# Decode attention with gated mix on one core: two V pairs loaded in halves, and the V sums in two PSUM tiles

## The chip, the core and the metric

One core of a Trainium2 chip. The metric is the device time of one execution in microseconds, lower is better; 2% is the threshold for "faster" or "slower". Engines: PE (TensorE matmul), PEld (its weight load), DVE (VectorE), ACT (ScalarE), POOL (GpSimd), SP (SyncE, which issues nearly all transfers here). The program uses one core. "Granted clock" is the share of its full clock at which PE was let run: 1.00 is called warm, 0.50 cold or half clock. PSUM is the memory, in banks, into which PE adds up its products. "Debt" is the time by which PE ends late because its own work, and not a transfer, holds it up. The "span" is the length of an execution as its profile shows it.

## The reference

Four decode queries attend over caches of 8192 positions and 32 heads; a small gated MLP runs beside it; the two results are mixed.

```
q      = (x @ wq)                                  # x [4,1,1024], 32 heads of 128
scores = q · k_cache * 128**-0.5                   # k_cache [4,32,8192,128] bf16, 256 MiB
o      = softmax(scores) · v_cache                 # v_cache the same size
a      = o @ wo                                    # wo [4096,1024], 8 MiB
b      = x + routed gated MLP(x)                   # w_gate, w_up, w_down 7 MiB each
out    = g * a + (1 - g) * b,   g = sigmoid(sum(x * gate_w))
```

Nearly all bytes, 512 MiB of 549, are the two caches.

## The kernel before

The caches come in "pairs": four heads, 8 MiB, two slots of a ring of five slots. K pairs 0 to 31 and V pairs run interleaved, V eight pairs behind; behind the last K pair only V pairs 24 to 31 (and 23) remain. A pair comes as one transfer, or as two halves where it wraps round the ring; the last three V pairs come in smaller pieces. PE adds a V pair in 64 matmuls into four PSUM banks; behind every second (odd) pair, ScalarE and VectorE add the four banks up into `OS`.

```python
def load_pair(src, n, apart=False):
    a = slots(2)
    if a + 1 < NS and not apart:              # one transfer of 8 MiB
        lo = a * RING
        nc.sync.dma_start(out=flat[:, lo:lo + 2 * n], in_=src)
        return [flat[:, lo:lo + n], flat[:, lo + n:lo + 2 * n]]
    halves = [ring[:, a], ring[:, (a + 1) % NS]]
    ...                                       # two transfers of 4 MiB

o_ps = accp.tile([P, 4, NB], F32, name="o_ps")   # four banks, one tile

def v_pair(d):
    flush_sums()
    if d < ND - 3:                            # ND = 32
        vs = load_pair(vv, RING)
    else:
        ...                                   # pairs 29 to 31: halves and smaller pieces
    for u in range(4 * RD):                   # 16 x 4 matmuls
        n, z = divmod(u, 4)
        vn = vs[n // JT]
        for w in range(4):
            nc.tensor.matmul(o_ps[row:row + NM, w, :], ...)
        if u == 1:
            flush()                           # small matmuls on OS
    if tv == GV - 1:                          # odd pairs
        sum_up(g, t, b, h0)

def sum_up(g, t, b, h0):
    nc.scalar.activation(out=OS[:], in_=o_ps[:, 0, :], func=ACT.Copy, scale=mE[:, 0:1])
    def sums():
        for w in range(1, 4):
            nc.vector.scalar_tensor_tensor(out=OS[:], in0=o_ps[:, w, :], scalar=mE[:, w:w + 1], in1=OS[:], ...)
    full.append(sums)
```

At the end: two blocks of `wo` (1 MiB each) ahead of pair 31, six behind it, the last two in pieces; each block is eight matmuls. Then a cast and the output transfer.

Of the kernel before, what the change touches and what calls it, by code (L numbers as in the profile page):

```python
# [9 lines left out]
F32 = mybir.dt.float32  # L10
U32 = mybir.dt.uint32
ACT = mybir.ActivationFunctionType
ALU = mybir.AluOpType
# [99 lines left out]
def kernel(  # L113
# [15 lines left out]
    nc = tc.nc  # L129
    P = 128  # L130
    Bn, Sq, D = A_x.shape
    _, H, Sk, Dh = A_k_cache.shape
# [8 lines left out]
    GD = QP // RD  # L141
    GH = GD * NQ
    ND = Bn * H // NQ
# [4 lines left out]
    FR = 4  # L148
    FG = F // (P * FR)
    NB = 512  # L150
    NH = D // NB
    RING = JR * Dh
# [3 lines left out]
    scale = float(Dh) ** -0.5  # L156
# [6 lines left out]
    accp = ctx.enter_context(tc.tile_pool(name="accp", bufs=1, space=PSUM))  # L163
# [14 lines left out]
    def turned(rows, n, dtype=BF):  # L178
        t = TB[tb_turn[0] % 3]
        tb_turn[0] += 1  # L180
        return t[0:rows, 0:n] if dtype == BF else t[0:rows, 0:2 * n].bitcast(dtype)

    def slots(n):
        at = turn[0]
        turn[0] = (at + n) % NS
        return at
# [3 lines left out]
    def load_pair(src, n, apart=False):  # L190

        a = slots(2)
        if a + 1 < NS and not apart:
# [4 lines that stand above are left out]
        for i, half in enumerate(halves):  # L198
            nc.sync.dma_start(out=half[:, 0:n], in_=src[:, i * n:(i + 1) * n])
        return halves  # L200


    S0 = scp.tile([P, 4, NB], F32, name="S_ps")
    o_ps = accp.tile([P, 4, NB], F32, name="o_ps")

    def bank(ps, z, shape, dtype=F32):
        b = ps[:, z] if dtype == F32 else ps[:, z].bitcast(dtype)
        n = 1
        for k in shape:
            n *= k  # L210
        names = "abcd"[:len(shape)]
        return b[:, 0:n].rearrange("p (%s) -> p %s" % (" ".join(names), " ".join(names)), **dict(zip(names, shape)))
# [8 lines left out]


    q_ps = S0[:, 0:2]
    for z in (q_ps, o_ps[:, 0:2], o_ps[:, 2:4]):
        nc.vector.memset(z, 0.0)

    row = const.tile([P, 2, 32], F32)
# [21 lines left out]
    for half in range(2):  # L249
        for e in range(2):  # L250
            nc.gpsimd.tensor_copy(out=R[:, 2 * half + e].rearrange("p (n j) -> p n j", n=4),
                                  in_=ident[:, 64 * half + e:64 * half + 64:2].unsqueeze(1).to_broadcast([P, 4, 32]))
# [7 lines left out]
    mE = const.tile([P, 4], F32)  # L260
# [9 lines left out]
    OS = const.tile([P, 4 * Dh], F32)  # L270
# [9 lines left out]
    A_ps = []  # L280
# [33 lines left out]
    def x_rows(ps, ws, nb, cols):  # L314

        for half, w in enumerate(ws):
            for t in range(TW):
                for k in range(4):
                    for z in range((nb - k + 3) // 4):
                        nc.tensor.matmul(ps[32 * k:32 * k + Bn, z, :], lhsT=xT[TW * half + t], rhs=cols(w, t, 4 * z + k),  # L320
                                         start=(half + t == 0), stop=(half == 1 and t == TW - 1), skip_group_check=True)
# [19 lines left out]
    def gu_piece(view, w_i):  # L341

        ws = load_pair(view.rearrange("(c t) f -> c (t f)", t=DT), TW * F)

        def cols(w, t, i):
            row = w[:, t * F:(t + 1) * F].rearrange("p (f i r) -> p f i r", i=FG, r=FR)
            return row[:, :, i, :]
        x_rows(o_ps[:, 2 * w_i:2 * w_i + 2], ws, FG, cols)

    def h_done():  # L350
        h = turned(P, 1024, F32).rearrange("p (z n) -> p z n", z=2)
        nc.scalar.activation(out=h, in_=o_ps[:, 0:2], func=ACT.Silu)
        nc.vector.tensor_tensor(out=h, in0=h, in1=o_ps[:, 2:4], op=ALU.mult)
        for z in range(2):
            ht = bank(o_ps, z, [FR, 4, 32])
            for r in range(FR):
                nc.tensor.transpose(out=ht[:, r].rearrange("p k i -> p (k i)"), in_=h[:, z, r:512:FR], identity=ident[:])
            kn = min(4, FG - 4 * z)
            for r in range(FR):
                nc.vector.tensor_tensor(out=hT[:, 4 * z:4 * z + kn, r, :], in0=ht[:, r, 0:kn, 0:Bn],  # L360
                                        in1=c12[:, 1:2, :].to_broadcast([P, kn, Bn]), op=ALU.mult)
# [46 lines left out]
    full = []  # L408
    ahead = []

    def flush():
        while pending:
            pending.pop(0)()

    def flush_sums():
        while full:
            full.pop(0)()

    def flush_late():
        while late:  # L420
            late.pop(0)()

    def heads(d):
        return divmod(d * NQ, H)

    def kv_view(cache, d):
        b, h0 = heads(d)
        return cache[b, h0:h0 + NQ].rearrange("h (r j) d -> (h r) (j d)", j=2 * JR)
# [86 lines left out]
    NM = 16 * NQ  # L515

    def v_pair(d):
        b, h0 = heads(d)
        g, t = divmod(d, GD)
        tv = t % GV  # L520
        row = NM * tv
        flush_sums()
        vv = kv_view(A_v_cache, d)
        if d < ND - 3:
            vs = load_pair(vv, RING)
        else:
            vs = [ring[:, slots(1)] for _ in range(2)]
            for half, cuts in ((0, 1), (1, 2)) if d < ND - 1 else ((0, 2), (1, 4)):
                for c in range(cuts):
                    lo, hi = c * RING // cuts, (c + 1) * RING // cuts  # L530
                    nc.sync.dma_start(out=vs[half][:, lo:hi], in_=vv[:, half * RING + lo:half * RING + hi])
        for u in range(4 * RD):
            n, z = divmod(u, 4)
            vn = vs[n // JT]
            for w in range(4):
                j0 = CJ * (n % JT) + 16 * z + 4 * w
                nc.tensor.matmul(o_ps[row:row + NM, w, :],  # L537
                                 lhsT=PB[:, RD * (d % NW) + n, z].rearrange("p w s j -> p (w s j)"),
                                 rhs=vn[:, j0 * Dh:(j0 + 4) * Dh], start=(u == 0), stop=(u == 4 * RD - 1),
                                 skip_group_check=True)  # L540
            if u == 1:
                flush()
            if u == 7:
                flush_late()
        if tv == GV - 1:
            sum_up(g, t, b, h0)
        if t < GD - NW:
            spread_p(d + NW)
        if t == GD - 1 and d + 1 < ND:
            spread_p(d + NW)  # L550

    def sum_up(g, t, b, h0):
        nc.scalar.activation(out=OS[:], in_=o_ps[:, 0, :], func=ACT.Copy, scale=mE[:, 0:1])  # L553

        def sums():
            for w in range(1, 4):
                nc.vector.scalar_tensor_tensor(out=OS[:], in0=o_ps[:, w, :], scalar=mE[:, w:w + 1], in1=OS[:],  # L557
                                               op0=ALU.mult, op1=ALU.add)
        full.append(sums)

        def finish():
            ps = A_ps[1] if A_ps else o_ps
            oT = bank(ps, 0, [HV])
            for q in range(4):
                nc.tensor.matmul(oT, lhsT=OS[:, q * Dh:(q + 1) * Dh], rhs=selg[:, q].rearrange("p t s -> p (t s)"),  # L565
                                 start=(q == 0), stop=(q == 3), skip_group_check=True)
            if t == GV - 1:
                tot = bank(ps, 1, [GH])
                nc.tensor.matmul(tot, lhsT=rs_t[g][:, 0:1].to_broadcast([P, P]), rhs=mask, start=True, stop=True, skip_group_check=True)

            def scaled():
                if t == GV - 1:
                    rinv_t[g] = stat.tile([P, GH], F32, name="rinv", tag="rinv")
                    nc.vector.reciprocal(out=rinv_t[g][:], in_=tot)
                hg = h0 + NQ - HV
                at = NQ * t + NQ - HV
                nc.vector.scalar_tensor_tensor(out=OT[:, hg:hg + HV, b], in0=oT, scalar=sgb[:, 1, b:b + 1],  # L577
                                               in1=rinv_t[g][:, at:at + HV], op0=ALU.mult, op1=ALU.mult)
            late.append(scaled)
        pending.append(finish)  # L580
# [3 lines left out]
    q_done()  # L584
    gates()
    gu_piece(B_w_gate, 0)
    side = {1: lambda: (gu_piece(B_w_up, 1), h_done())}
    GE = NWB - HV // WB
    order = []
# [70 lines left out]
```

## Time and profile before

| | before |
|---|---|
| time, median of 3 runs | 1343.73 us (1342.73 to 1343.86) |
| time of the run whose profile was read | 1345.62 us |
| span of that profile | 1343.8 us |
| transfers' share of the span | 99.3% |

The chain that ended last shows how the end came about (start, length, what):

```profile
1229.08 29.40 DMA ring<-in_A_v_cache_dram
1258.48 0.14 issue
1258.62 2.56 PE o_ps L537 x8
...
1335.71 5.14 PE acc L286 x23
```

From the landing of pair 28 at 1258.48 on, the end follows PE (and the sums that it waits for), and no transfer. The other lines of this profile are in the prediction.

### The profile page before, as it was taken

The numbers are of one execution on the slowest core, as the hardware profiler recorded it, in microseconds if no ns is written. First come the engines' busy times: TensorE is split into PE (matmuls) and PEld (weight loads), VectorE is DVE, ScalarE is ACT, GpSimd is POOL, SyncE is SP. The second block draws the span as 40 slices with busy tenths as digits, with TensorE's granted clock in tenths as the row PEclk, the third lists the DMA queues.
The fourth block names the chain that finished last, engine by engine and source line by source line (L and its number), as shares of the span: only waits on it lengthen the run. The fifth ranks groups of instructions, "written<-read, shape, count | busy, mean of one in ns | idle before, by whom it ended". The sixth has DMA issues, their size and how long they took to land.

```text
span 1343.8 us, 6898 instructions
## 1 busy us (share of the span) xinstructions
PE 1063.6 (79%) x4608; PEld 139.9 (10%) x1396; DVE 638.9 (48%) x386; ACT 63.3 (5%) x94; POOL 71.6 (5%) x209
## 2 busy tenths in 40 slices
PE   2665877897878789787879778789588878888898
PEld 0000000011010011101001010101001010111111
DVE  2555988556544347455436256646135556000001
ACT  0000000200000000100000000100000000100000
POOL 2000000100000001000000000100000000100000
PEclk9687999898989899888889889889898889888889
DMA  9999999999999999999999999999999999999997
GB/s 414 445 421 436 438 433 423 444 434 423 438 437 425 435 435 427 440 436 430 435 432 431 437 435 422 436 429 434 437 424 445 433 422 436 434 424 438 424 425 303
DMA packets 14602, 576.13 MB, mean 429 GB/s; under 512 B 1630, under 2 KB 1638, under 8 KB 2284
## 3 DMA queue, kind: packets, MB, share of 16 engines
q1 hardware_dynamic: 14564, 575.69, 99.3%
q8 instruction: 23, 0.38, 0.1%
q14 instruction: 7, 0.06, 0.0%
q10 hardware_dynamic: 8, 0.00, 0.0%
HBM read 575.68 MB, written 0.01 MB: 428 GB/s over the span
## 4 chain that ended last, share of the span: by engine, by line
DMA 59%; DVE 23%; PE 16%; another core or an unknown queue 1%; issue 0%; ACT 0%; SPq 0%; DVEq 0%
DMA ring<-in_A_k_cache_dram 51%; DVE TB L453 20%; PE o_ps L537 12%; DMA ring<-in_A_v_cache_dram 7%; DVE OS L557 2%; PE S_ps L458 2%; DMA x<-in_gate_w_dram 2%; PE acc L286 1%; PE led L565 0%; PE S_ps L320 0%; DVE PT L494 0%; DVE mx L480 0%; ACT OS L553 0%; PE o_ps L565 0%
## 5 line engine op out<-in xcount | busy, mean ns | idle before, releaser
L453 DVE STREAM_TRANSPOSE TB<-ring 128x2048 uint32<-128x2048 uint32 x256 | 568.1, 2277 | 472.2 <-DMA ring<-in_A_k_cache_dram 453.6
L458 PE MATMUL S_ps<-TB,Z 128*128 128x512 bf16 x2048 | 530.5, 413 | 189.1 <-DVE TB L453 181.5
L537 PE MATMUL o_ps<-ring,PB 128*64 128x512 bf16 x2048 | 469.7, 392 | 48.9 <-DMA ring<-in_A_v_cache_dram 39.5
L458 PEld LDWEIGHTS <-Z 128*128 128x128 bf16 x512 | 53.0, 103 | 651.7 <-issue 651.7
L537 PEld LDWEIGHTS <-PB 128*64 128x64 bf16 x512 | 57.7, 113 | 453.2 <-issue 452.5
L557 DVE SCALAR_TENSOR_TENSOR OS<-o_ps,mE,OS 128x512 f32<-128x512 f32 x48 | 35.6, 741 | 141.6 <-ACT OS L553 140.5
L513 POOL COPY PB<-PT 32x256 bf16<-32x256 bf16 x64 | 39.0, 609 | 720.3 <-PE o_ps L537 527.2
L511 ACT COPY PB<-PT 32x256 bf16<-32x256 bf16 x64 | 39.6, 618 | 254.3 <-PE o_ps L537 248.5
L435 POOL COPY Z<-qa 32x4 bf16<-32x4 bf16 x128 | 25.7, 201 | 458.5 <-PE S_ps L458 432.0
L553 ACT ACTIVATE OS<-o_ps,mE 128x512 f32<-128x512 f32 x16 | 11.0, 687 | 592.1 <-PE o_ps L537 592.1
L489 ACT ACTIVATE TB<-S_ps,mx 128x2048 bf16<-128x2048 f32 x4 | 7.9, 1967 | 321.2 <-DVE mx L486 321.2
L286 PE MATMUL acc<-ring,hT 128*4 128x512 bf16 x56 | 14.2, 421 | 5.4 <-ACT TB L489 5.4
L244 PE MATMUL S_ps<-identb,x 6*128 6x6 bf16 x8 | 0.6, 195 | 22.2 <-DMA x<-in_gate_w_dram 22.2
L286 PE MATMUL acc<-ring,LT 128*4 128x512 bf16 x64 | 14.4, 379 | 0.4 <-DVE LT L383 0.4
L320 PE MATMUL o_ps<-ring,xw 128*4 128x512 bf16 x112 | 10.1, 483 | 4.6 <-DMA ring<-in_B_w_gate_dram 4.6
L565 PEld LDWEIGHTS o_ps<-selg,OS 128*128 128x128 f32 x88 | 11.5, 191 | 9.4 <-issue 9.0
L494 DVE STREAM_TRANSPOSE PT<-TB 128x2048 bf16<-128x2048 bf16 x4 | 9.2, 2311 | 6.4 <-ACT TB L489 6.4
L480 DVE TENSOR_REDUCE mx<-S_ps 128x1 f32<-128x2048 f32 x4 | 9.1, 2281 | 6.2 <-PE S_ps L458 6.2
L565 PE MATMUL o_ps<-selg,OS 128*128 128x8 f32 x88 | 10.5, 245 | 0.0
L577 DVE SCALAR_TENSOR_TENSOR OT<-led,sgb,rinv 128x8 bf16<-128x8 f32 x5 | 1.2, 236 | 15.4 <-PE led L565 15.3
L383 DVE CAST LT<-led 128x96 bf16<-128x96 f32 (+1 forms) x2 | 0.4, 224 | 15.9 <-PE led L381 15.9
L246 DVE COPY xw<-S_ps 128x48 bf16<-128x48 bf16 x1 | 0.2, 181 | 15.7 <-PE S_ps L244 15.7
(68 smaller groups left out, 73.6 us busy)
## 6 DMA issues: line engine op xcount, KB each, us to landing
ring<-in_A_k_cache_dram SPq DMA_DIRECT2D x14, 4096.0 KB, 33.4
ring<-in_A_v_cache_dram SPq DMA_DIRECT2D x14, 4096.0 KB, 28.9
ring<-in_A_v_cache_dram SPq DMA_DIRECT2D x6, 2048.0 KB, 26.7
ring<-in_B_w_gate_dram SPq DMA_DIRECT2D x1, 7168.0 KB, 37.1
ring<-in_B_w_up_dram SPq DMA_DIRECT2D x1, 7168.0 KB
ring<-in_B_w_down_dram SPq DMA_DIRECT2D x1, 7168.0 KB
ring<-in_A_wo_dram SPq DMA_DIRECT2D x6, 1024.0 KB, 26.4
ring<-in_A_v_cache_dram SPq DMA_DIRECT2D x4, 1024.0 KB, 27.0
```

The costliest lines, as they stand in the source:

```text
L286: nc.tensor.matmul(acc(n), lhsT=lhsT, rhs=rhs, start=start, stop=True, skip_group_check=True)
L320: nc.tensor.matmul(ps[32 * k:32 * k + Bn, z, :], lhsT=xT[TW * half + t], rhs=cols(w, t, 4 * z + k), start=(half + t == 0), stop=(half == 1 ...
L435: nc.gpsimd.tensor_copy(out=Z[at, :, QP - 1 + QP * q], in_=qa[at, :, h0 + q, b])
L453: nc.vector.transpose(out=flat_t.bitcast(U32).rearrange("p (j i) -> p j i", j=CJ), in_=kn[:, half].bitcast(U32))
L458: nc.tensor.matmul(sps[:, z, :], lhsT=Z[:, 2 * half + e, s:s + P], rhs=T[:, 16 * z:16 * z + 16, :, e], start=(t + n + half + e == 0), stop ...
L494: nc.vector.transpose(out=PT[:].rearrange("p j i -> p (j i)"), in_=PTs)
L511: nc.scalar.copy(out=Bv[at, :, :, q, :], in_=Pv[at])
L513: nc.gpsimd.tensor_copy(out=Bv[at, :, :, q, :], in_=Pv[at])
L537: nc.tensor.matmul(o_ps[row:row + NM, w, :], lhsT=PB[:, RD * (d % NW) + n, z].rearrange("p w s j -> p (w s j)"), rhs=vn[:, j0 * Dh:(j0 + 4 ...
L553: nc.scalar.activation(out=OS[:], in_=o_ps[:, 0, :], func=ACT.Copy, scale=mE[:, 0:1])
L557: nc.vector.scalar_tensor_tensor(out=OS[:], in0=o_ps[:, w, :], scalar=mE[:, w:w + 1], in1=OS[:], op0=ALU.mult, op1=ALU.add)
L565: nc.tensor.matmul(oT, lhsT=OS[:, q * Dh:(q + 1) * Dh], rhs=selg[:, q].rearrange("p t s -> p (t s)"), start=(q == 0), stop=(q == 3), skip_ ...
```

## The change

Intent: PE should begin pairs 26 to 28 as soon as half of each has landed, and should stand less behind each odd pair: ScalarE empties one tile of two banks while VectorE empties the other, and the next pair may begin in the first tile when ScalarE is done.

```diff
-    o_ps = accp.tile([P, 4, NB], F32, name="o_ps")
+    o_ps = [accp.tile([P, 2, NB], F32, name=f"o_ps{i}") for i in range(2)]
@@ v_pair
-            vs = load_pair(vv, RING)
+            vs = load_pair(vv, RING, apart=d >= ND - GD + 2)
-                nc.tensor.matmul(o_ps[row:row + NM, w, :],
+                nc.tensor.matmul(o_ps[w // 2][row:row + NM, w % 2, :],
@@ sum_up (new argument d; up to pair 22 as before, on the new tiles)
+        if d < ND - GD - 1:
+            ...
+        else:
+            half = [OS[:], turned(P, 4 * Dh, F32)]
+            for w in range(2):
+                nc.scalar.activation(out=half[w], in_=o_ps[0][:, w, :], func=ACT.Copy, scale=mE[:, w:w + 1])
+            for w in range(2):
+                nc.vector.scalar_tensor_tensor(out=half[w], in0=o_ps[1][:, w, :], scalar=mE[:, 2 + w:3 + w], in1=half[w],
                                                op0=ALU.mult, op1=ALU.add)
+            nc.vector.tensor_tensor(out=OS[:], in0=half[0], in1=half[1], op=ALU.add)
```

(The other hunks rename `o_ps[:, 0:2]` to `o_ps[0]` and the like.) Pair 26 wraps round the ring and came in halves before, so only pairs 27 and 28 are loaded differently.

More of the change, by code (lines that the diff above doesn't have):

```diff
@@ L223 @@
     q_ps = S0[:, 0:2]
-    for z in (q_ps, o_ps[:, 0:2], o_ps[:, 2:4]):
+    for z in (q_ps, o_ps[0][:], o_ps[1][:]):
         nc.vector.memset(z, 0.0)
@@ L347, in cols @@
             return row[:, :, i, :]
-        x_rows(o_ps[:, 2 * w_i:2 * w_i + 2], ws, FG, cols)
+        x_rows(o_ps[w_i], ws, FG, cols)
     def h_done():
         h = turned(P, 1024, F32).rearrange("p (z n) -> p z n", z=2)
-        nc.scalar.activation(out=h, in_=o_ps[:, 0:2], func=ACT.Silu)
-        nc.vector.tensor_tensor(out=h, in0=h, in1=o_ps[:, 2:4], op=ALU.mult)
+        nc.scalar.activation(out=h, in_=o_ps[0][:], func=ACT.Silu)
+        nc.vector.tensor_tensor(out=h, in0=h, in1=o_ps[1][:], op=ALU.mult)
         for z in range(2):
-            ht = bank(o_ps, z, [FR, 4, 32])
+            ht = bank(o_ps[z], 0, [FR, 4, 32])
             for r in range(FR):
@@ L545, in v_pair @@
         if tv == GV - 1:
-            sum_up(g, t, b, h0)
+            sum_up(d, g, t, b, h0)
         if t < GD - NW:
@@ L550, in v_pair, with sum_up, sums @@
             spread_p(d + NW)
-    def sum_up(g, t, b, h0):
-        nc.scalar.activation(out=OS[:], in_=o_ps[:, 0, :], func=ACT.Copy, scale=mE[:, 0:1])
-        def sums():
-            for w in range(1, 4):
-                nc.vector.scalar_tensor_tensor(out=OS[:], in0=o_ps[:, w, :], scalar=mE[:, w:w + 1], in1=OS[:],
+    def sum_up(d, g, t, b, h0):
+        if d < ND - GD - 1:
+            nc.scalar.activation(out=OS[:], in_=o_ps[0][:, 0, :], func=ACT.Copy, scale=mE[:, 0:1])
+            def sums():
+                for w in range(1, 4):
+                    nc.vector.scalar_tensor_tensor(out=OS[:], in0=o_ps[w // 2][:, w % 2, :], scalar=mE[:, w:w + 1], in1=OS[:],
+                                                   op0=ALU.mult, op1=ALU.add)
+            full.append(sums)
+        else:
[4 more added lines that the diff above has]
+                nc.vector.scalar_tensor_tensor(out=half[w], in0=o_ps[1][:, w, :], scalar=mE[:, 2 + w:3 + w], in1=half[w],
                                                op0=ALU.mult, op1=ALU.add)
-        full.append(sums)
+            nc.vector.tensor_tensor(out=OS[:], in0=half[0], in1=half[1], op=ALU.add)
         def finish():
-            ps = A_ps[1] if A_ps else o_ps
+            ps = A_ps[1] if A_ps else o_ps[1]
             oT = bank(ps, 0, [HV])
```

## The prediction

> **What bounds the kernel now.** I read the page first, then the chain that ended last in order of time, then the timelines of the last 190 us, and the table of stretches for the last 14 us. The page says that the stream of transfers is full:
>
> ```profile
> DMA packets 14602, 576.13 MB, mean 429 GB/s; under 512 B 1630, under 2 KB 1638, under 8 KB 2284
> q1 hardware_dynamic: 14564, 575.69, 99.3%
> ```
>
> 576 MB at 429 GB/s is 1343 us, the whole span. Nothing in the diff takes a byte away, so a big gain is out of the question; only what happens after the last byte can shrink. The table of stretches shows when that is (columns: stretch, length, busy us and instruction counts of PE, PEld, DVE, ACT, POOL, then granted clock, DMA share, GB/s):
>
> ```profile
> 1336.00:1337.00 1.00, 1.00 (x6) 0.17 (x2) 0.00 (x0) 0.00 (x0) 0.00 (x0) 1.00 0.26 98
> 1337.00:1338.00 1.00, 1.00 (x6) 0.26 (x3) 0.00 (x0) 0.00 (x0) 0.00 (x0) 1.00 0.00 0
> 1338.00:1339.00 1.00, 1.00 (x7) 0.17 (x2) 0.00 (x0) 0.00 (x0) 0.00 (x0) 1.00 0.00 0
> ```
>
> The last input byte lands at about 1337.1 us. The PE timeline of the tail:
>
> ```profile
> 1239.18 15.66 PE L537 MATMUL o_ps<-ring,PB 128*64 128x512 bf16 x64 [3.23 <-DMA ring<-in_A_v_cache_dram]
> 1258.62 2.56 PE L537 MATMUL o_ps<-ring,PB 128*64 128x512 bf16 x8 [3.78 <-DMA ring<-in_A_v_cache_dram]
> 1261.11 1.88 PE L565 MATMUL led<-selg,OS 128*128 128x8 f32 x8
> 1262.91 26.58 PE L537 MATMUL o_ps<-ring,PB 128*64 128x512 bf16 x120
> 1292.63 2.45 PE L537 MATMUL o_ps<-ring,PB 128*64 128x512 bf16 x8 [3.14 <-DVE OS L557]
> 1295.01 1.88 PE L565 MATMUL led<-selg,OS 128*128 128x8 f32 x8
> 1296.82 14.15 PE L537 MATMUL o_ps<-ring,PB 128*64 128x512 bf16 x56
> 1315.18 14.00 PE L537 MATMUL o_ps<-ring,PB 128*64 128x512 bf16 x64
> 1335.71 5.12 PE L286 MATMUL acc<-ring,LT 128*4 128x512 bf16 x23
> ```
>
> 64 matmuls are one V pair: these are pairs 27, 28 and 29 (8 + 120), 30 (8 + 56) and 31. From 1258.62 to the end PE waits for no transfer: it runs late behind the stream, with one hole of 3.14 us after pair 29 and one of 0.41 us, and ends at 1340.83, 3.7 us after the last byte. Then come the casts and the output transfer, to 1343.8: 3.0 us that the change doesn't touch. So the end is set by PE since 1258.62, and that start was set by pair 28, one transfer of 8 MB. The part that the transfers hide is everything before.
>
> The sums, from the timelines of ScalarE and VectorE behind pair 29:
>
> ```profile
> 1289.53 0.69 ACT L553 ACTIVATE OS<-o_ps,mE 128x512 f32<-128x512 f32 x1 [32.83 <-PE o_ps L537]
> 1290.25 2.33 DVE L557 SCALAR_TENSOR_TENSOR OS<-o_ps,mE,OS 128x512 f32<-128x512 f32 x3 [26.99 <-ACT OS L553]
> ```
>
> 0.69 + 2.33 and three handovers are the 3.14 us in which PE stands, because all four banks are one tile.
>
> **What the skill says.** "TensorE: Matmul & The Clock Gate", Part 1, says that PE falls to half clock after an idle window of about 3.4 us, free-running, and needs about as long to come back. The trace agrees in kind: after the hole of 3.14 us the mean clock of 1293 to 1300 is 0.56, after the 3.78 us at 1258 it is 0.55 for 7 us, and even an idle of 2.23 us at 1198 gave 0.58 for 4 us. The price after pair 29: 2.45 + 1.88 + 14.15 = 18.5 us for what pair 26 does warm at 1.75 (8 of its warm 12.27 / 56) + 1.06 + 12.27 = 15.1 us: 3.4 us. "PSUM — Partial Sum Buffer", Specifications, says that ScalarE and VectorE may read PSUM in parallel as long as they are in different banks; the kernel before never does so, so its trace can't tell. "DMA: Bandwidth & Descriptors", "Why a DMA increments its semaphore by 16 and not by 1", says that a transfer is shared by up to 16 engines that finish independently and only the full count means landed; the slope at the end (397, 389, 332, 252, 231, 176, 98, 0 GB/s in the microseconds from 1330 to 1338) fits engines that end at different times. Hence the last engine, not the mean rate, sets 1337.1.
>
> **The change, part by part.** (1) Halves. Of pairs 26 to 28, pair 26 wraps round the ring of five slots and comes in halves already (two issues on the wrap line at 1178.56), and the order of issues shows only pairs 27 and 28 changed: two issues become four, no byte more. Landings, as an estimate: pair 28 lands at 1258.48 (the chain: 29.40 us from 1229.08), and 32 MiB follow (pairs 29 to 31 and 8 MiB of wo) until 1337.1, that is 2.457 us per MiB. So half of pair 28 lands at 1248.8, half of 27 at about 1229.5; then pair 29 at 1268.3, 1273.2, 1278.1 (half, two quarters), pair 30 at 1287.9, 1292.9, 1297.8, two wo blocks by 1302.7, pair 31 in six pieces from 1307.6 to 1322.3, wo blocks 2 to 5 at 1324.8, 1327.3, 1329.7, 1332.2, and the pieces of 6 and 7 at 1333.4, 1334.6, 1335.9, 1336.5, 1337.1. These do not move: the stream has no hole to fill.
>
> (2) Sums. In the new order ScalarE reads two banks and waits only for the last matmul into them, two matmuls (0.44 us) before the pair ends; two reads of 0.69 end 0.94 us after it. PE's first two matmuls wait for ScalarE alone and take 0.44. VectorE's second sum starts at about 0.97 and ends 0.75 later, at 1.72; the third matmul waits for that. PE stands 0.94 + 0.34 = 1.3 us instead of 3.14, in two short holes, which should leave the clock up (a hole of 1.66 us in the K stage was followed by eight matmuls in 1.96 us, the same as after 0.23 us). The new add of the two halves (some 0.6 us, an estimate from the 0.75 of a sum) lies behind VectorE's reads; the matmuls that need it come eight matmuls later. On the other stages, the K pairs and pairs before 23, the instructions of every engine are the same but for waits.
>
> (3) PE with both. Pair 27 can run from about 1232 to 1246.5; pair 28's first half from 1248.8 (cold, 8.7 us plus 1.1 for the small matmuls), its second from its landing, to 1265.8; pair 29 from 1268.3 in pieces to about 1284; sums; pair 30 from 1287.9, cold, to 1304.5; two wo blocks (3.6) to about 1309; pair 31 pieces keep up from there, the last (1322.3) ends at 1324.1; wo 2 and 3 end at 1329.1, with the last sum beside them; small matmuls 1.0, wo 4 by 1331.9, the last LT copy 0.5, wo 5 by 1334.2, block 6 by 1336.0, block 7: the last piece from 1337.25, two matmuls, 1337.7. PE has then no debt left; it ends 0.6 us after the last byte in place of 3.7. Sum: 1340.83 − 1337.7 = 3.1 us. The time is 1343.7 − 3.1 = 1340.6; I put 0.2 on it for a late or half-clocked matmul: 1340.8, or 0.2% less.
>
> The two parts aren't additive. Halves alone still have the 3.14 us after pair 29, but that lies before 1287.9, when pair 30 lands: about 1341. Sums alone leave pair 28's start at 1258.5, but take 1.8 + 3.4 = 5.2 us out behind pair 29, more than the 3.1 us of debt: also about 1341.
>
> **The rivals.** Transfers hidden anyway: if the stream set the end already, 1343.7 would stay. For it: 99.3%. Against: 3.7 us of PE after the last byte, with no wait for a transfer since 1258.62. A slower stream: more and smaller transfers could lose rate; each us lost moves the end by one. Against: issues on the wrap line wait 12 times on VectorE and 11 times on PE, so many pairs come in halves already, within the same 414 to 445 GB/s of the page's slices; I would give this 0 to 1 us. A better stream: slots come free earlier and issues stand earlier; the stretch 1252 to 1255 has 317 GB/s and share 0.73, some 0.8 us lost. If that came from late issues, the end would be near 1340.0; but pair 28's issue at 1229.08 stood ten us ahead of the landing of pair 27, so the queue wasn't dry. PE lagging still: if waits for pieces keep throwing the clock to half, pair 31 and the last blocks (15 us warm) cost up to 2 us more, of which the end sees about half, since the last blocks run at 1.8 us against 2.46 us per MiB: 1341.8. A longer last sum: the added 0.6 us would lie behind pair 31, but 16 matmuls of wo (3.6 us) stand beside a chain of about 2.5 us.
>
> **Range and chances.** The three runs of before spread over 1.1 us, the rivals over 1339.8 to 1343.7. I take 1339.6 to 1343.2. 2% is 27 us, eight times the debt: within 2% is all but certain.
>
> **What would show it.** Right: PE waits for transfers in pair 30, pair 31 and the last blocks; its last matmul ends within 1 us of the last byte; the last byte stays at 1337 ± 1; behind odd pairs ScalarE has two reads and PE a hole of about 1 us and a shorter one; no 3 us holes on sums. Wrong: the last byte moves by over 1.5 us; PE's last 23 matmuls run without a wait again; or the clock after pair 29's sums is still near half.

## The result, and the profile after

Changed kernel: 1343.26 us median of six runs (1343.15 to 1343.46). Kernel before beside it: 1342.99 us median of six (1342.54 to 1343.86). Ratio 1.0001, 95% interval 0.9988 to 1.0014: the same. The class "within 2%" was right; the number, 1340.8 us, was 2.5 us too low, and the median lies 0.06 us above the upper end of the range.

The profile after is of a run of 1343.33 us, with a span of 1341.4. Against the span before, 1343.8, that is 2.4 us less, so in the two profiles the change looks like most of the gain of 3.1 us that was forecast. The stream, from the page:

```profile
DMA packets 14890, 576.13 MB, mean 429 GB/s; under 512 B 1662, under 2 KB 1670, under 8 KB 2316
q1 hardware_dynamic: 14852, 575.69, 99.5%
```

The bytes and the rate are unchanged. PE in the tail (start, length, engine, line, operation, count, and in brackets the idle time before it and its releaser):

```profile
1249.40 2.19 PE L537 MATMUL o_ps<-ring,PB 128*64 128x512 bf16 x8 [1.06 <-DMA ring<-in_A_v_cache_dram]
1259.02 7.07 PE L537 MATMUL o_ps<-ring,PB 128*64 128x512 bf16 x32 [1.15 <-DMA ring<-in_A_v_cache_dram]
1268.73 13.97 PE L537 MATMUL o_ps<-ring,PB 128*64 128x512 bf16 x64 [2.65 <-DMA ring<-in_A_v_cache_dram]
1288.33 3.48 PE L537 MATMUL o_ps<-ring,PB 128*64 128x512 bf16 x8 [5.63 <-DMA ring<-in_A_v_cache_dram]
1325.22 1.89 PE L286 MATMUL acc<-ring,LT 128*4 128x512 bf16 x8 [0.60 <-DMA ring<-in_A_wo_dram]
1332.69 5.64 PE L286 MATMUL acc<-ring,LT 128*4 128x512 bf16 x24
```

Before, PE waited for no transfer after 1258.62. Now it waits for each: for both halves of pair 28, for pairs 29 and 30, and for the wo blocks. It has caught up with the stream. Its last matmul ends at 1338.33 instead of 1340.83. The stretches at the end show that the last byte has moved by no more than a fraction of a microsecond (columns as in the prediction; DMA share and GB/s are last):

```profile
1336.00:1337.00 1.00, 0.86 (x5) 0.10 (x2) 0.00 (x0) 0.00 (x0) 0.00 (x0) 1.00 0.36 139
1337.00:1338.00 1.00, 1.00 (x7) 0.17 (x2) 0.00 (x0) 0.00 (x0) 0.00 (x0) 1.00 0.02 6
```

In stretches of 0.1 us the last input bytes are seen up to 1336.7 us before and up to 1337.2 us after. PE ended 4.1 us behind the last byte before (the prediction read 1337.1 and 3.7 us off stretches of 1 us), and 1.1 us behind it after.

The sums behind pair 29, from the timelines of ScalarE and VectorE:

```profile
1282.31 0.69 ACT L564 ACTIVATE OS<-o_ps,mE 128x512 f32<-128x512 f32 x1 [31.95 <-PE o_ps L537]
1282.90 0.68 ACT L564 ACTIVATE TB<-o_ps,mE 128x512 f32<-128x512 f32 x1
1283.03 0.75 DVE L566 SCALAR_TENSOR_TENSOR OS<-o_ps,mE,OS 128x512 f32<-128x512 f32 x1 [30.18 <-ACT OS L564]
1283.70 0.74 DVE L566 SCALAR_TENSOR_TENSOR TB<-o_ps,mE,TB 128x512 f32<-128x512 f32 x1
```

ScalarE's second read and VectorE's first run side by side in different banks at 0.68 and 0.75 us, as long as one alone (0.69 and 0.75 to 0.76 before). "PSUM — Partial Sum Buffer", Specifications, says that they can; this trace agrees. Both are done 2.1 us after ScalarE began, in place of 3.05. The chain of the changed kernel ends with a transfer:

```profile
1320.28 16.12 DMA ring<-in_A_wo_dram
1336.40 0.04 issue
1336.44 1.90 PE acc L286 x8
```

So every mechanism is there, and yet the median time has not moved. Where is the gain? The question is no longer what the change did in the profile, but whether the profile of before stood for the kernel before.

### The profile page after: what moved, and what is told of

Read it like the earlier page. It is cut to its first block, busy times and chain, and to the rows that moved or that the text cites. A ratio compares the mean times of both kernels' runs of the same rounds, so it can differ in the third digit from the quotient of the medians.

```text
span 1341.4 us, 6922 instructions
## 1 busy us (share of the span) xinstructions
PE 1057.9 (79%) x4608; PEld 138.4 (10%) x1396; DVE 638.3 (48%) x386; ACT 66.2 (5%) x99; POOL 71.8 (5%) x209
## 2 busy tenths in 40 slices
DMA packets 14890, 576.13 MB, mean 429 GB/s; under 512 B 1662, under 2 KB 1670, under 8 KB 2316
## 4 chain that ended last, share of the span: by engine, by line
DMA 67%; DVE 21%; PE 11%; issue 0%; ACT 0%; SPq 0%; DVEq 0%
DMA ring<-in_A_k_cache_dram 51%; DVE TB L453 19%; DMA ring<-in_A_v_cache_dram 12%; PE o_ps L537 7%; PE S_ps L458 3%; DMA ring<-in_B_w_gate_dram 3%; DVE OS L558 2%; DMA ring<-in_A_wo_dram 1%; PE o_ps L320 0%; DVE PT L494 0%; DVE mx L480 0%; PE acc L286 0%; PE led L574 0%; PE o_ps L574 0%; DVE OS L566 0%
## 5 line engine op out<-in xcount | busy, mean ns | idle before, releaser
L537 PE MATMUL o_ps<-ring,PB 128*64 128x512 bf16 x2048 | 462.8, 388 | 50.3 <-DMA ring<-in_A_v_cache_dram 49.0
L566 DVE SCALAR_TENSOR_TENSOR OS<-o_ps,mE,OS 128x512 f32<-128x512 f32 x5 | 3.8, 750 | 138.9 <-ACT OS L564 138.9
L558 DVE SCALAR_TENSOR_TENSOR OS<-o_ps,mE,OS 128x512 f32<-128x512 f32 x33 | 24.3, 737 | 1.5
```

Of the source, the lines that this page charges most:

```text
L537: nc.tensor.matmul(o_ps[w // 2][row:row + NM, w % 2, :], lhsT=PB[:, RD * (d % NW) + n, z].rearrange("p w s j -> p (w s j)"), rhs=vn[:, j0 ...
L558: nc.vector.scalar_tensor_tensor(out=OS[:], in0=o_ps[w // 2][:, w % 2, :], scalar=mE[:, w:w + 1], in1=OS[:], op0=ALU.mult, op1=ALU.add)
```

## The experiments

Twelve runs were made. They are of ten kernels: e1, e9 and e10 are the kernel before again, e2 the changed one. "Late" kernels (e5, e6, e12: more work for PE) and "short" ones (e7, e8: fewer bytes) probe how much slack PE has against the stream. The theories that the expectations name: S says that the debt differs from run to run and was large in the profile of before; R, H and L are its rivals, and C is S with the half clock as the cause.

### e1, e2: both kernels again

No edit. Five timed rounds each.

> The kernel before, once more, for its spread. Theory S (the profile of before is a slow sample: its own run took 1345.62 against 1342.99 for the median of six): the times lie at 1342.5 to 1344, ratio 1.000, and this profile has a span near 1341 to 1342 with the last 23 matmuls ending under 2.5 us after the last byte, instead of 3.7. Rival R (the debt of 3.7 us is in every run, and the changed kernel lost 3 us elsewhere): the profile shows a span near 1343.8 again, or a span of 1341 with the same 3.7 us behind an earlier last byte.

> The changed kernel, once more. S: times within 1343.1 to 1343.5, ratio to before 0.999 to 1.001, span about 1341.3, PE ends 0.6 to 1.5 us after the last byte. R: the same times, but a last byte that lies later than that of e1 by 1.5 us or more.

| | median | range | profiled run: time, span | ratio to before (95%) |
|---|---|---|---|---|
| e1 (before) | 1343.82 | 1342.69 to 1345.91 | 1344.62, 1342.8 | 0.9997 (0.9983 to 1.0011) |
| e2 (after) | 1343.26 | 1343.11 to 1344.00 | 1343.81, 1341.8 | 0.9994 (0.9982 to 1.0007) |

The kernel before beside them: 1343.57 median of eleven, 1342.57 to 1347.03. So before has a wide spread, wider than S expected (1344), and the changed kernel a narrow one (up to 1344.00, where 1343.5 was expected). e1's profile fell again in a longish run, with a span of 1342.8 where theory S expected 1341 to 1342: its last 23 matmuls end at 1339.86, 2.4 us after the last byte (1337.5 in stretches of 0.1 us). The debt is there, but smaller than in the first profile (4.1 us behind the last byte, read in the same way): it varies. In e2 the last byte comes at 1337.7, only 0.2 us later than in e1, so rival R falls.

### e3, e4: each half of the change alone

```diff
# e3, on the kernel before
-            vs = load_pair(vv, RING)
+            vs = load_pair(vv, RING, apart=d >= ND - GD + 2)
# e4, on the changed kernel
-            vs = load_pair(vv, RING, apart=d >= ND - GD + 2)
+            vs = load_pair(vv, RING)
```

> Kernel before with pairs 27 and 28 in halves, sums as before. S: pair 28 starts near 1249, debt gone, PE waits for pair 30's transfer in spite of the 3.1 us hole after pair 29; time 1342.8 to 1343.5, ratio 1.000. R: if smaller transfers cost the stream rate, the last byte and the time are later by 1 us or more than e1 and as late as e2.

> Changed kernel with pairs 27 and 28 whole again. S: pair 28 starts near 1258.5 as in before; the hole behind pair 29 shrinks from 3.1 to about 1.2 us; PE ends under 2 us after the last byte; time 1342.5 to 1343.5. R: if the second ScalarE read or the added sum cost something, later than e1 by 1 us or more.

e3: 1343.05 us (1342.92 to 1344.32), ratio 0.9993 (0.9980 to 1.0006). e4: 1343.24 us (1342.93 to 1343.98), ratio 0.9993 (0.9981 to 1.0006). Both profiles have a span of 1341.1, and in both PE waits for wo blocks at the end. In e3 pair 28 began at 1254.61 rather than at 1249, because pair 27 ran until 1251.5 and the hole for its sums came first; behind pair 29 PE did not wait for pair 30's transfer but for the 3.13 us of sums, which differs from what was expected. In e4 the holes behind pair 29 were 0.92 and 0.28 us. Either half suffices to pay the debt, and each ends where both end.

### e5, e6: 24 matmuls more at the head of pair 29

```diff
-            for w in range(4):
+            for w in (range(4) if (d, u) != (ND - 3, 0) else 7 * list(range(4))):
```

The first group of pair 29 is done seven times; each restarts its bank, so the result stays right.

> Kernel before with 24 extra matmuls (5.2 us warm) at the head of pair 29; the result stays right. Theory S (in before PE carries a debt behind the stream that varies from run to run, from nearly 0 to some 4 us): nothing absorbs the 5.2 us, the time rises by 4 to 5.2 us, to about 1347.5. Rival H (transfers hide PE in before as well, and the spread comes from the stream itself): it rises by less than 1 us.

> The same 24 matmuls in the changed kernel. S: they fit into the wait for pair 30 (5.63 us in the profile of after, 3.93 in e2), the time rises by 0 to 0.5 us, to 1343.3 to 1343.8. Rival: if the changed kernel has no slack to speak of, it rises by 4 us or more, as before does.

Before with them: 1349.88 us (1345.85 to 1352.82), ratio 1.0035 (1.0016 to 1.0054), which is 4.7 us of 5.2. The median lies 2.4 us above the 1347.5 that was expected: six runs with a spread of 7 us fix the rise only roughly. Changed kernel with them: 1343.74 us (1343.41 to 1344.30), 0.5 us above 1343.26 in e2 on another chip, ratio to before 0.9995 (0.9981 to 1.0009). The PE timeline of e6 shows where they went:

```profile
1269.06 19.15 PE L537 MATMUL o_ps<-ring,PB 128*64 128x512 bf16 x88 [2.66 <-DMA ring<-in_A_v_cache_dram]
1289.14 0.59 PE L537 MATMUL o_ps<-ring,PB 128*64 128x512 bf16 x2 [0.92 <-ACT TB L564]
1290.00 1.46 PE L537 MATMUL o_ps<-ring,PB 128*64 128x512 bf16 x6 [0.28 <-DVE TB L566]
```

Pair 30 begins at 1289.14 instead of 1288.33, in place of a wait of 5.63 us, and finds the clock up. PE again ends 1.1 us after the last byte. So the changed kernel has some 5 us of slack here. The kernel before has next to none in its long runs (highest 1352.82 with the extra work, 1347.50 without) and some 2 us in its quick ones (lowest 1345.85 and 1342.69, 3.2 us of 5.2).

### e7, e8: 2 MiB of pair 29 left out

```diff
-                for c in range(cuts):
+                for c in range(cuts if (d, half) != (ND - 3, 1) else 1):
```

The result is wrong; all matmuls stay and read what an earlier pair left there.

> Kernel before without the second quarter-pair transfer of pair 29 (2 MiB, 4.9 us of the stream; the result is wrong on purpose, the matmuls stay). S: PE is late from pair 28 on, so fewer bytes behind pair 28 help little: the fast runs fall by 0 to 2 us, the slow ones not at all. H: it falls by 4 to 4.9 us.

> The same 2 MiB left out in the changed kernel (wrong on purpose). S: PE has the slack to follow, the end is set by the last byte: the time falls by 4 to 4.9 us, to about 1338.8, and is faster than e7 by 2 us or more. H: it falls as much as e7 does.

Before, shortened: 1340.98 us (1340.69 to 1343.63), ratio 0.9979 (0.9964 to 0.9994), 2.8 us less on the means. Changed, shortened: 1338.39 us (1338.21 to 1339.05), ratio to the kernel before 0.9956 (0.9942 to 0.9970), 5.9 us less. The changed kernel follows the stream by the full 4.9 us (from 1343.26 in e2, on another chip, to 1338.39); before follows by about half, and is 2.6 us slower than the shortened changed kernel. The quickest run of before fell by 2.0 us (1342.69 beside it, 1340.69), as expected; its long runs, which were expected to stay, fell as well (highest 1343.63 of five runs, against 1347.50 of eleven). So the end of the changed kernel is set by the last byte, and that of before by PE in the long runs. For the quick runs the profile of e7 (1340.98 us, within 0.3 us of its quickest) says more. Here PE keeps the full clock through pair 30 in spite of the hole (the first line), and works to its end without waiting for a transfer (the last):

```profile
1291.30 1.89 PE L537 MATMUL o_ps<-ring,PB 128*64 128x512 bf16 x8 [3.13 <-DVE OS L557]
1331.13 5.13 PE L286 MATMUL acc<-ring,LT 128*4 128x512 bf16 x23
```

Its own work ends at 1336.26. With all bytes, an end that is set by transfers lies at 1338.06 (e3), so as an estimate a quick run of before has 1.8 us of slack and no debt. That fits the 2.0 us by which the quickest run fell and the 2 us of slack in e5.

### e9, e10: two more looks at the kernel before

No edit; only a profile and one time each.

> The kernel before once more, one look, in the hope of a profile of one of its quick runs (1342.6 to 1343.1; about half of them are). Theory C (the debt of PE varies with how much of pairs 28 to 30 falls to the half clock after the holes, 0 to 3.4 us per hole): a quick run ends its last 23 or 24 matmuls within 1.5 us of the last byte and takes pair 28 and 29 in about 29 us and pair 30 with its small matmuls in about 15.1 us, as the profile of e7 has them; a slow one takes 31 us or more and 18 us. Rival L (the landings vary): the warm times are the same in quick and slow runs and the landing of pair 28 moves.

> The kernel before, one look, a second try at a quick run. C: quick (under 1343.1) goes with about 29 us for pairs 28 and 29 and 15.1 us for pair 30; slow (over 1344) with 31 us or more, or with 18 us for pair 30. L: no such link.

Both fell in long runs, 1346.70 and 1345.81 us, so no quick run was seen in a profile. But they show what varies. First e9, then e1, the same kernel:

```profile
1258.62 3.59 PE L537 MATMUL o_ps<-ring,PB 128*64 128x512 bf16 x8 [5.47 <-DMA ring<-in_A_v_cache_dram]
1293.74 2.38 PE L537 MATMUL o_ps<-ring,PB 128*64 128x512 bf16 x8 [3.14 <-DVE OS L557]
1296.04 1.88 PE L565 MATMUL led<-selg,OS 128*128 128x8 f32 x8
1297.85 14.22 PE L537 MATMUL o_ps<-ring,PB 128*64 128x512 bf16 x56
```

```profile
1294.90 1.89 PE L537 MATMUL o_ps<-ring,PB 128*64 128x512 bf16 x8 [3.13 <-DVE OS L557]
1296.72 1.06 PE L565 MATMUL led<-selg,OS 128*128 128x8 f32 x8
1297.70 12.27 PE L537 MATMUL o_ps<-ring,PB 128*64 128x512 bf16 x56
```

The hole behind pair 29 is the same 3.13 to 3.14 us in both; pair 30 with its small matmuls then takes 18.3 us in e9 (and in e10) and 15.1 us in e1. The mean granted clock of the 7 us from 1294 is 0.57 in e9; from 1295 it is 1.00 in e1. In e7 that hole cost nothing either, and the one behind pair 27 (also 3.13 us) only about a third as much as in e1 (its 8, 8 and 120 matmuls end 29.0 us after their start, against 32.2 us in e1 and 27.6 us in e11 below, at full clock). The landing of pair 28 does not decide it: PE starts pair 28 at 1258.62 both in the first profile (1345.62 us) and in e9 (1346.70 us). The link between time and clock that was expected for long runs is there; that a quick run has the warm times is not shown by a profile of one. But the record has the mean granted clock of every run, over its whole span: it is 0.903 to 0.909 in the 9 runs of before that took over 1345 us (mean 0.905), and 0.907 to 0.913 in the 16 that took under 1343.2 us (mean 0.910). Over all 37 timed runs of before, time and clock have a correlation of −0.69.

### e11: the holes filled, nothing else changed

```diff
         if tv == GV - 1:
             sum_up(g, t, b, h0)
+        if d in (ND - 5, ND - 3):
+            for i in range(14):
+                nc.tensor.matmul(A_ps[1][0:NM, 1, :], lhsT=PB[...], rhs=vn[:, j0 * Dh:(j0 + 4) * Dh],
+                                 start=True, stop=True, skip_group_check=True)
```

The kernel before, with 14 idle matmuls into a bank that nobody reads, behind pairs 27 and 29. Transfers and sums are untouched, the result is right.

> Kernel before with 14 matmuls (3.0 us) into an unused bank in the holes behind pairs 27 and 29; the result stays right, the sums and transfers are as before. C: the clock after pair 29 no longer falls, pair 30 with its small matmuls takes 15.1 us, PE's start is not later by more than 0.3 us; the slow runs vanish in part: spread under 1.5 us, median 1342.7 to 1343.3, no run above 1344.5. L: the spread of 1342.6 to 1347.5 stays, median near 1343.8.

1342.84 us (1342.56 to 1343.76), against 1343.67 (1342.56 to 1345.72) of nine runs of before; ratio 0.9998 (0.9984 to 1.0011). No run is long, as C expected; five runs are few, though: 12 of 43 timed runs of before lie above 1344 us, so five below it in a row would come by chance about one time in five. What the matmuls changed is seen in the profile. PE in e11, at pair 28 and at pair 30:

```profile
1258.87 1.89 PE L537 MATMUL o_ps<-ring,PB 128*64 128x512 bf16 x8 [1.91 <-DMA ring<-in_A_v_cache_dram]
1289.64 1.89 PE L537 MATMUL o_ps<-ring,PB 128*64 128x512 bf16 x8 [1.38 <-DVE OS L561]
1292.44 12.27 PE L537 MATMUL o_ps<-ring,PB 128*64 128x512 bf16 x56
```

From the table of stretches, behind pair 29, first e9, then e11:

```profile
1294.00:1301.00 7.00, 7.00 (x24) 2.36 (x12) 0.24 (x1) 0.00 (x0) 0.00 (x0) 0.57 1.01 422
```

```profile
1290.00:1297.00 7.00, 7.00 (x38) 1.73 (x15) 0.23 (x1) 0.00 (x0) 0.00 (x0) 1.00 0.99 418
```

With nearly the same bytes per microsecond, 38 matmuls go through at clock 1.00 where 24 went at 0.57. Pair 28 starts 0.25 us later than in e9, and the run ends 3.8 us earlier. So the half clock after the holes, and not the landing of pair 28, made the debt. L is not wrong in everything: the last byte moves as well (see below).

### e12: halves alone, with the 24 matmuls of e5

> Kernel before with pairs 27 and 28 in halves and the 24 extra matmuls of e5 at the head of pair 29: how much of the slack of e6 the halves give alone. From the profile of e3: pair 29 ends at 1285.5 + 5.2, plus 3.1 for the sums, 1293.8, 5.5 us after pair 30's first half lands; of these the stream gives back some 2.5 us until the end: 1345 to 1347.5. If it stays under 1344, the sums' two tiles add no slack.

1343.72 us (1343.20 to 1344.19), ratio 1.0003 (0.9991 to 1.0016). The expectation was wrong: the halves alone absorb the 5.2 us, and by its own terms the two tiles then add no slack that this test can see. It was worked out from e3's profile, whose pair 28 began at 1254.61; in e12's it began at 1251.62.

## Why the prediction was right or wrong

**What held, by its own steps.** That the time stays within 2% held. The bound on the stream held: 576.13 MB at 429 GB/s in both profiles. The schedule of PE held closely: pair 28 from 1248.8 forecast and 1249.40 measured, its second half from 1258.5 and 1259.02, pair 29 from 1268.3 and 1268.73, pair 30 from 1287.9 and 1288.33, the last matmul at 1337.7 and 1338.33. The holes at the sums held: 0.94 + 0.34 us forecast, 0.92 + 0.27 us measured behind pair 25, where no transfer hid them, and the mean clock from 1216 to 1222 was 1.00. The claim that the two parts aren't additive held: each alone (e3, e4) does what both do. Of the rivals, a better stream did not appear, and smaller transfers did not slow the stream beyond the 1.0 us by which its end differs anyway (1336.7 to 1337.7 in the profiles with all bytes). One of the signs of being wrong did appear: the clock in pair 30 still fell to half (18.3 us for pair 30 in e2), behind a wait for a transfer, as its schedule had it ("pair 30 from 1287.9, cold"). It cost nothing, since PE had the slack: the change did not take the half clock away but moved it to where PE waits anyway.

**The step that failed** is this one: "The time is 1343.7 − 3.1 = 1340.6". It takes a debt read from one profile off the median of other runs. That profile's own run took 1345.62 us. Taken from that, 3.1 us gives 1342.5, and the profiled run after took 1343.33. The two numbers looked alike by chance: 1343.73 as a median time, and 1343.8 as the span of a run that was 1.9 us longer than the median. Had the 1.8 us between span and time been used, the forecast span of 1340.7 (1337.7 for PE's end and the 3.0 us behind it) would have been written down as a time of 1342.5. With this goes the first rival, "Transfers hidden anyway": it was set aside because of the debt in the one profile, and it describes the quick runs. Smaller slips: the last byte was at 1336.7, not at 1337.1 (that it came at 1337.2 in the profile after is luck); PE ends 1.1 us after it and not 0.6; and at 2.457 us per MiB half of pair 27 lands at 1229.0 and half of pair 28 at 1248.65, a few tenths before the times given.

**What stood in its place.** Over the 37 runs of before that e1 and the timed rounds brought, 16 took 1342.56 to 1343.13, 12 took 1343.57 to 1344.62, and 9 took 1345.62 to 1347.50. PE's end lies 4.8 us before the time in every profile of before (1345.62 − 1340.83, 1344.62 − 1339.86, 1346.70 − 1341.95). As an estimate from this, a run of 1342.6 has PE's end at 1337.8, about a microsecond after the last byte, where the ends that are set by transfers lie: in nearly half of its runs the kernel before then pays no debt at all. The debt arises when the half clock falls on pairs 27 to 30 (in e1 pair 27 took 16.5 us rather than the 14.0 of e9, and with the hole behind it set the start of pair 28). The prediction knew the price (3.4 us behind pair 29) and took it for fixed, although the same page of the skill, "TensorE: Matmul & The Clock Gate", Part 1, calls the window free-running and warns that its phase differs from run to run. The runs agree: the same hole of 3.13 us cost 3.2 us in e9 and nothing in e1.

**Where the expected gain went.** Off the path in the quick runs, where the stream sets the end; kept in the long ones, of which none was seen with the change. Nothing of 11 runs of the changed kernel lies above 1344.00, where before has 12 of its 43 timed runs (the 37 and the six beside the result). The medians differ by tenths: of the 37 runs, 16 had nothing to gain, and the 12 in the middle lie only 0.3 to 1.4 us above the 1343.26 of the changed kernel. e6 and e8 show what the change bought: some 5 us of slack of PE against the stream at pair 29, which would become time only if the stream were shorter.

**What stays open.** The half clock is not the whole spread. In the profiles in which transfers set the end, PE ends 1.0 to 1.2 us after the last byte, and that byte comes at 1337.0 in e3, e4 and e11 (1342.92 to 1343.09 us) and at 1337.5 to 1337.7 in e2, e6 and e12 (1343.72 to 1343.81 us). So some tenths come from the stream itself, in kernels with and without the change; how much of the middle group of before is this and how much debt, and why the stream ends later in some runs, is not shown. The quickest runs of before (1342.54) and of e11 (1342.56) are half a microsecond below the quickest of the changed kernel (1343.11). Some 0.2 us of this lies outside the span: the time is 1.74 to 1.86 us longer than the span in the 66 runs with both, of kernels with the old sums, and 1.83 to 2.14 us in the 26 of kernels with the new sums (means 1.80 and 1.98); the cause was not looked for. No profile of a quick run of the unaltered kernel before was caught. e11 has the lowest median, 1342.84, but its interval against before holds 1.0, so no version is shown to beat the others in the mean. In spread, the changed kernel, e3, e4 and e11 together have no run of 26 above 1344.32 us, where before has 10 of 43; five runs of one kernel don't rank them.

## What to carry to other kernels

Before a debt is read from a profile, look at the time of the very run that was profiled, and whether it is an ordinary one; a span and a time aren't the same measure (here they lie 1.7 to 2.1 us apart), and a difference is to be taken between like and like. Holes of a few microseconds in PE's work can be followed by half-clock matmuls in one run and not in the next (3.2 us or nothing behind the same hole here), so a change that fills the holes, or gives PE slack behind them, may narrow the spread and leave the median nearly alone. When the stream of transfers is full, test what a change bought by adding work to the other engine and by taking bytes away: the slack shows, even where the time does not.

## What the Trainium skill lacked or had wrong

- "TensorE: Matmul & The Clock Gate", Part 1, gives the rule that idle gaps over about 3.4 us bring the half clock. Shorter ones did as well: a hole of 2.23 us before pair 25 was followed by a mean clock of 0.58 from 1201 to 1205, and holes of 3.13 to 3.14 us by 0.57 (e9) or by 1.00 (e1). In these runs, then, a gap under 3.4 us did not always keep the full clock.
- The same page says that the ramp costs under 1% of a typical kernel and should not be fitted. It is under 1% here too, but it makes the long runs of before (3.2 us behind one hole, of a spread of 1342.54 to 1347.50 us); with 14 matmuls in each of two holes (e11) five runs took 1342.56 to 1343.76.
- How the time of a run relates to the span that its profile shows would belong to "Runtime: NRT & Kernel Launch"; no figure for these two was found there. The time was 1.7 to 2.1 us longer in every run here that has both (1345.62 and 1343.8, 1343.33 and 1341.4, 1343.81 and 1341.8).
